# Attention outputs of a unit in one step and two PSUM banks, with the last keys' four products on the four quarters of TensorE

## The chip, the cores and the metric

The kernel runs on one NeuronCore of a Trainium2 chip. The metric is the device time of one execution in microseconds (us), as the median of several runs. The engines are named as in the profile: PE is TensorE (PEld its weight loads), DVE is VectorE, ACT is ScalarE, POOL is GpSimd, SP is SyncE. PE writes its results into PSUM banks; ACT here moves them to SBUF.

## The reference

Two blocks follow each other. The first is attention that keeps only the 32 best keys of every query, for 8 batches of 8 heads with 576 positions and 64 dimensions:

```python
scores = scale * np.matmul(q, k.transpose(0, 1, 3, 2))
kth = np.partition(scores, -top_k, axis=-1)[..., -top_k:-top_k + 1]
scores = np.where(scores >= kth, scores, -1000000000.0)
attn = np.exp(scores - np.max(scores, axis=-1, keepdims=True))
attn = attn / (np.sum(attn, axis=-1, keepdims=True) + 1e-09)
x = np.matmul(attn, v)
```

The second sends each of the 4608 rows of `x` (512 wide) to the one expert of eight with the largest logit, computes `relu(x @ w1[e]) @ w2[e]` there (512 to 1024 to 512), and scales the row with the gate's probability. Everything is float32.

## The kernel before

**Units, tiles, steps.** A unit is a pair of heads: the 128 partitions hold 64 dimensions of each, so there are 8 x 4 = 32 units. The 576 queries of a head are four tiles of 128 and a tail of 64. One step of the main loop (`loop`, 144 steps) works on two score tiles side by side, the same tile number of both heads; the two tails of an even and of the odd unit behind it form one step together. So two units take nine steps. By their place in these nine, steps 0 to 3 are the tiles of the even unit, step 4 is the tails, steps 5 to 8 are the tiles of the odd unit (`groups`, line 252).

**What a step does.** DVE searches the 32nd largest score of each query (`fold`, `fold_on`, `search`). ACT then forms `low` from the threshold (line 401) and a mask term with two Relu passes (line 417); POOL subtracts it from the scores (`less`, line 426); ACT takes the exponential (line 434). PE turns the weights of the step before (`transposed`: eight transposes `wTm`, line 445, and one or two for the last 64 keys, `wTl`, lines 459 and 461), ACT copies them out of PSUM (`wT`, lines 450 and 452; `wTt`, lines 467 and 469), and PE makes the scores of the step four ahead (`products`, line 304), which ACT copies to `s` (line 311) one step later.

**Order of work.** The order on PE, ACT and DVE is the program order of `loop`, written by hand; POOL's operations are held in program order too (`in_turn`). Within a step ACT's order is: `low`, Relu, copies of scores, then what is due at the place "relu" (copies of outputs), copies of turned weights, exponentials, and last the copy of `wTt`. PE's order is: the eight transposes, some pieces, the transpose for the last keys, more pieces, the scores, what is due at the place "products" (outputs), and the rest of the pieces. A piece is a fragment of the expert blocks, four matmuls of line 979 or one of line 996; `share` decides how the pieces that a step may have are spread over the places of the nine, and a step's share is cut in three by `part = min(BETWEEN, now - now // 2)` and `now // 2`. What is left of the experts' work runs after the loop, on PE alone.

**Outputs.** When a unit's weights are turned, `outputs` multiplies them with V. For each half of 288 queries there are five chunks of keys and two heads: ten matmuls, each 64 output rows wide, so that the two heads stand on the two column halves of the array. The fifth chunk is the last 64 keys of both heads, one head above the other on the partitions; V has zeros in its place for the other head, so that a product over all 128 partitions gives one head's sum (`_laid_out`). Each half takes one bank, ACT copies it to `oT` (line 484), and later five products with a turning matrix (`px`, line 493) bring rows and logits. `ending` places these: for the even unit the first half at the end of step 3 and the second at the end of step 5; for the odd unit at the end of step 8 and of the next step 0; `px` is one step after the second half.

**Banks.** Outputs, turned weights, `px` and the ranks of the gate share one pool of two banks (`bank`, tag "t"). Each new user waits until the copy out of the bank two users ago is done.

Of the kernel before, what the change touches and what calls it, by code (L numbers as in the profile page):

```python
# [44 lines left out]
def kernel(  # L45
# [205 lines left out]

    def groups(u):

        first, second = ([((a, i), (a, NC + i)) for i in range(NC)] for a in (u, u + 1))
        return first + [((u, 2 * NC), (u + 1, 2 * NC))] + second

    def in_turn(put):
# [14 lines left out]

    def tails(tiles):
        return tiles[0][1] == 2 * NC

    def tail_at(n):
        return 0 if n.u % 2 else S
# [80 lines left out]
    def search(tiles, s, f, then=lambda: None, soon=False, behind=lambda: None, beside=lambda: None):  # L358

        m_all = range(2)  # L360
        tops = k.small.tile([P, 2, TOP_K], F32, name="tops", bufs=4)
        if k.exact:
            src = [s[:, m, :, :].rearrange("p j k -> p (j k)") for m in m_all]
            width = S
        else:
            src = [f.few[:, m, 0:QF] for m in m_all]
            width = LW
            if not f.aside:
                lists(f)
        behind()  # L370
        scr = k.att.tile([P, 2, width], F32, name="scr", bufs=1)
        nbias = k.small.tile([P, 2], F32, name="nbias", bufs=3)
        R = TOP_K // 8

        for r in range(R):
            if r == R - 1 and not soon:
                then()
            for m in m_all:
                nc.vector.max(out=tops[:, m, r * 8:(r + 1) * 8], in_=src[m])  # L379
                if r > 1:  # L380
                    tick()
            if r == 1 and soon:
                then()
            if r == 0:
                in_turn(nc.gpsimd.tensor_scalar_mul(nbias, tops[:, :, 0], -scale))
                beside()
            if r < R - 1:
                for m in m_all:
                    first = r == 0 and not k.exact
                    nc.vector.match_replace(  # L390
                        out=src[m] if first else scr[:, m, :], in_to_replace=tops[:, m, r * 8:(r + 1) * 8],
                        in_values=src[m], imm_value=NEG,
                    )
# [7 lines left out]
        nc.scalar.activation(low, thr, AF.Copy, scale=STEEP)  # L401

        def doubts():
            n, i = tiles[0]
# [25 lines left out]
    def weights(tiles, w, nbias):  # L430

        for m, (n, i) in enumerate(tiles):
            c = 2 * NC if tails(tiles) else 2 * tiles[0][1] + m
            nc.scalar.activation(  # L434
                w[:, m, :], w[:, m, :], AF.Exp, scale=scale, bias=nbias[:, m:m + 1], accum_out=n.z[:, c:c + 1]
            )

    def transposed(tiles, w):

        q = slice(ST + tiles[0][1] * P, ST + (tiles[0][1] + 1) * P)  # L440
        for m, (n, i) in enumerate(tiles):
            pm = bank("wTm")
            for c in range(NC):
                first = c * P + (0 if tails(tiles) else m * ST)
                nc.tensor.transpose(pm[:, c * P:(c + 1) * P], w[:, m, first:first + P], ident)  # L445
            pm4 = pm[:, :].rearrange("p (c q) -> p c q", c=NC)
            if tails(tiles):
                at = tail_at(n)
                pmh = pm4.rearrange("p c (h q) -> p c h q", h=2)
                nc.scalar.copy(wT[:, :, :, at:at + ST], _turned(pmh, 2) if m else pmh)  # L450
            else:
                nc.scalar.copy(wT[:, :, m, q], pm4)  # L452
                if k.between and not m:
                    yield
        yield
        pt = bank("wTl")
        if tails(tiles):
            for a in range(2):
                nc.tensor.transpose(pt[0:ST, a * P:(a + 1) * P], w[:, 1 - a, SM:S], ident)
        else:  # L460
            nc.tensor.transpose(pt[:, 0:P], w[:, :, :].rearrange("p m k -> p (m k)")[:, SM:SM + P], ident)
        yield
        if tails(tiles):
            pt4 = pt[0:ST, 0:2 * P].rearrange("p (r q) -> p r q", q=ST)
            for h in range(2):
                both = wTt[h * ST:(h + 1) * ST, :].rearrange("p (a q) -> p a q", q=ST)[:, 0:NT + 1:NT, :]
                nc.scalar.copy(both, pt4[:, 0:4:3, :] if h else pt4[:, 1:3, :])
        else:
            nc.scalar.copy(wTt[:, q], pt[:, 0:P])

    def outputs(n, x):

        odd = n.u % 2
        oT = oT_of[odd]
        for j in range(2):
            q = slice(j * HF + (0 if odd else ST), (j + 1) * HF + (0 if odd else ST))
            po = bank("po")
            for c in range(KC):
                for h in range(2):
                    r = slice(h * D, (h + 1) * D)  # L480
                    rhs = wT[:, c, h, q] if c < NC else wTt[:, q]
                    nc.tensor.matmul(po[r, 0:HF], n.v[:, c, r], rhs, start=(c == 0), stop=(c == KC - 1))  # L482
            yield
            nc.scalar.copy(oT[:, j * HF:(j + 1) * HF], po[:, 0:HF])  # L484
            yield
        starts = [t * P + (ST if odd else 0) for t in range(NC)] + [0 if odd else SM]
        xw = P + lw
        n.xl = k.small.tile([P, KC, xw], F32, name="xl", bufs=1)
        put = []
        for t0, t1 in ((0, KC - 2), (KC - 2, KC)):  # L490
            px = bank("px")
            for t in range(t0, t1):
                nc.tensor.matmul(
                    px[:, (t - t0) * xw:(t - t0 + 1) * xw], oT[:, starts[t]:starts[t] + P],
                    turn[:, n.u // 2, odd * lw:odd * lw + xw], start=True, stop=True,
                )
# [527 lines left out]
    with fast:  # L1024
# [86 lines left out]
        def ending(b, u):  # L1111
# [6 lines left out]
                lg_of[b] = k.small.tile([P, KC, E], F32, name="lg")  # L1118
            x, lg = x_of[b], lg_of[b]
            out_steps = outputs(n, x)  # L1120
            yield "products"
            next(out_steps)
            yield "relu"
            next(out_steps)
            if u % 2 == 0:
                yield "relu"
            div = divisors(n)
            next(div)
            aside.append(div)
# [95 lines left out]
        def multiply(i):  # L1225
            tiles = tiles_of(i)
            got_of[i] = products(tiles, i < AHEAD)
            n, tile = tiles[0]
            more = n.b * U + n.u + 2
            if tile == (NC - 1 if n.u % 2 else 2 * NC) and more < len(units):  # L1230
                unit.append(load_unit(*units[more]))

        def loop():
# [15 lines left out]
            fold_on(f_of[0])  # L1249
            for i, (b, g) in enumerate(work):  # L1250
                tiles = tiles_of(i)
                u, tile = g[0]
# [37 lines left out]
                if b == B - 1 and at >= ARRIVED:  # L1290
                    room -= KEEP
                    credit = room / (len(work) - i)
                share = {0: 0.5, 1: 1.2, 2: 1.6, 3: 0.5, 2 * NC: 1.4}[tile]
                now = max(0, min(int(credit * share + 0.5), room))
                credit -= now
                clock = i
# [29 lines left out]
            assert len(late) == 1  # L1326
            clock = None
            for place in late[0][0]:
                if place == "rows":
                    pieces(4)  # L1330
            kept = left - (SURE + HALVES + PLAIN) * PIECES
            assert kept >= 0, kept
            k.apart = True
# [24 lines left out]
    with ExitStack() as outer:  # L1358
# [10 lines left out]
        with ExitStack() as st:  # L1369
# [7 lines left out]
            with tc.For_i(0, B, 1) as b:  # L1377
# [3 lines left out]
                for u in range(0, U, 2):  # L1381
# [4 lines left out]
                    for g in groups(u):  # L1386
# [10 lines left out]
                        n, tile = tiles[0]  # L1397
# [33 lines left out]
def _laid_out(inputs):  # L1431
# [5 lines left out]
    T = S % P  # L1437
    qt, kt = (a.transpose(0, 1, 3, 2).reshape(B, U, P, S) for a in (q, k))
    vt = v.reshape(B, U, 2, S, D).transpose(0, 1, 3, 2, 4)
    vp = _np.zeros((B, U, S + T, 2, D), v.dtype)  # L1440
    vp[:, :, :S - T] = vt[:, :, :S - T]
    for h in range(2):
        vp[:, :, S + (h - 1) * T:S + h * T, h] = vt[:, :, S - T:, h]
    return {
        "qk": _np.concatenate([qt, kt[..., -T:], kt], axis=3),
        "v": vp.reshape(B, U, S + T, P),
# [27 lines left out]
```

## Time and profile before

| | |
|---|---|
| median of 3 runs | 1282.69 us (1282.21 to 1283.14) |
| the profiled execution | 1284.61 us, its span 1283.0 us |
| 20 to 220 us: PE, DVE, ACT busy | 142.09, 200.00, 168.28 us; PE clock 0.85 |
| 220 to 470 us | 227.38, 249.76, 217.51 us of 250; clock 0.96 |
| 470 to 1050 us | 567.76, 575.55, 495.94 us of 580; clock 1.00 |
| 1050 to 1283 us | 226.38, 18.24, 44.75 us of 233; clock 1.00 |

The first row of stages is attention alone, the next two are attention with the pieces of experts between it, the last is experts alone. The times of PE's matmuls overlap, and their ends are modelled, so the distance from one start to the next says what a matmul costs.

### The profile page before, as it was taken

The numbers are of one execution on the slowest core, as the hardware profiler recorded it, in microseconds if no ns is written. First come the engines' busy times: TensorE is split into PE (matmuls) and PEld (weight loads), VectorE is DVE, ScalarE is ACT, GpSimd is POOL, SyncE is SP. The second block draws the span as 40 slices with busy tenths as digits, with TensorE's granted clock in tenths as the row PEclk, the third lists the DMA queues.
The fourth block names the chain that finished last, engine by engine and source line by source line (L and its number), as shares of the span: only waits on it lengthen the run. The fifth ranks groups of instructions, "written<-read, shape, count | busy, mean of one in ns | idle before, by whom it ended". The sixth has DMA issues, their size and how long they took to land. (4 is left out here: it accounts for less than half of the span.)

```text
span 1283.0 us, 24461 instructions
## 1 busy us (share of the span) xinstructions
PE 1176.1 (92%) x7574; PEld 823.6 (64%) x7574; DVE 1058.8 (83%) x4608; ACT 933.3 (73%) x2136; POOL 732.0 (57%) x884
## 2 busy tenths in 40 slices
PE   6767767898899999999999999999999999999998
PEld 3444444665566566667666666666666667789975
DVE  8999999999999999999999999999999965000000
ACT  4888887988799888888788888888888872112121
POOL 4777777786678665658555855676557743101010
PEclk9888788999899999999999999999999999999999
DMA  5001113741474147533946464547555548996582
GB/s 153 31 30 31 31 39 126 263 157 39 146 251 162 39 150 283 182 135 98 332 142 218 163 224 153 189 146 264 178 178 202 172 149 285 353 358 235 215 301 83
DMA packets 98701, 220.81 MB, mean 172 GB/s; under 512 B 5309, under 2 KB 26301, under 8 KB 98560
## 3 DMA queue, kind: packets, MB, share of 16 engines
q1 hardware_dynamic: 91360, 198.87, 44.5%
q0 software_dynamic: 6384, 19.97, 4.2%
q8 instruction: 61, 1.00, 0.3%
q14 instruction: 80, 0.66, 0.2%
q10 hardware_dynamic: 816, 0.31, 0.1%
HBM read 195.75 MB, written 24.04 MB: 171 GB/s over the span
## 5 line engine op out<-in xcount | busy, mean ns | idle before, releaser
L426 POOL TENSOR_TENSOR w<-s,w 128x576 f32<-128x576 f32 x288 | 409.2, 1441 | 317.5 <-ACT w L417 317.4
L979 PE MATMUL ph<-xTs,w 128*128 128x128 f32 x2112 | 263.0, 278 | 2.6 <-ACT xTs L870 2.6
L979 PEld LDWEIGHTS ph<-xTs,w 128*128 128x128 f32 x2112 | 251.3, 194 | 21.1 <-issue 17.6
L996 PE MATMUL py<-w,hT 128*128 128x512 f32 x528 | 248.7, 600 | 1.9 <-ACT hT L984 1.6
L434 ACT ACTIVATE w<-w,nbias 128x576 f32<-128x576 f32 x288 | 223.0, 785 | 2.3 <-POOL w L426 1.4
L445 PE MATMUL wTm<-turn,w 128*128 128x128 f32 x1152 | 173.9, 291 | 52.7 <-ACT oT L484 29.1
L417 ACT ACTIVATE w<-s,low 128x576 f32<-128x576 f32 x288 | 207.7, 768 | 4.7
L304 PE MATMUL sc<-qkb 64*128 64x288 f32 (+1 forms) x1280 | 200.7, 465 | 7.8 <-DMA qkb<-in_qk_dram 4.0
L445 PEld LDWEIGHTS wTm<-turn,w 128*128 128x128 f32 x1152 | 135.1, 148 | 111.6 <-ACT oT L484 35.5
L311 ACT COPY s<-sc 128x576 f32<-128x576 f32 x288 | 168.0, 634 | 11.9 <-PE sc L304 11.8
L379 DVE MAX8 tops<-scr 128x8 f32<-128x168 f32 x576 | 169.5, 328 | 0.0
L452 ACT COPY wT<-wTm 128x512 f32<-128x512 f32 x256 | 140.7, 596 | 37.8 <-PE wTm L445 37.2
L379 DVE MAX8 tops<-few 128x8 f32<-128x144 f32 (+1 forms) x576 | 154.9, 314 | 0.0
L304 PEld LDWEIGHTS sc<-qkb 64*128 64x128 f32 (+1 forms) x1280 | 107.1, 190 | 71.5 <-issue 35.2
L996 PEld LDWEIGHTS py<-w,hT 128*128 128x128 f32 x528 | 92.0, 191 | 86.5 <-issue 83.0
L482 PE MATMUL po<-wT,vb 128*64 128x288 f32 x1024 | 143.8, 425 | 0.0
L888 POOL DMA_INDIRECT out_dram<-y,xg x37 | 38.9, 1052 | 161.3 <-ACT y L1005 82.0
L356 DVE MAX8 few<-l 128x8 f32<-128x288 f32 x288 | 129.8, 451 | 0.0
L320 DVE TENSOR_TENSOR h<-s 128x576 f32<-128x576 f32 (+1 forms) x145 | 111.7, 770 | 3.9 <-ACT s L311 3.6
L321 DVE TENSOR_TENSOR l<-s 128x576 f32<-128x576 f32 (+1 forms) x145 | 114.3, 788 | 0.0
L482 PEld LDWEIGHTS po<-wT,vb 128*64 128x64 f32 x1024 | 70.1, 141 | 68.9 <-issue 17.4
L356 DVE MAX8 few<-hl 128x8 f32<-128x72 f32 x576 | 102.3, 221 | 0.0
(205 smaller groups left out, 1596.7 us busy)
## 6 DMA issues: line engine op xcount, KB each, us to landing
w<-in_moe_w_dram SPq DMA_DIRECT2D x74, 2048.0 KB, 9.2
qkb<-in_qk_dram SPq DMA_DIRECT2D x31, 608.0 KB, 3.8
vb<-in_v_dram SPq DMA_DIRECT2D x32, 320.0 KB, 3.2
xg<-x_rows SPq DMA_DIRECT2D x37, 257.0 KB, 9.1
x_rows<-blank SPq DMA_DIRECT2D x13, 257.0 KB, 7.9
x_rows<-blank POOLq DMA_DIRECT2D x4, 257.0 KB, 9.8
x_rows<-x,posi POOLq DMA_INDIRECT x40, 3.2
out_dram<-y,xg POOLq DMA_INDIRECT x37, 3.9
```

The source lines that it names most:

```text
L304: nc.tensor.matmul(ps[rows, j, 0:HF], n.q[d, cols], n.k[d, keys], start=True, stop=True)
L311: lambda m=m, ps=ps: nc.scalar.copy(s[:, m, :, :], ps[:, :, 0:HF]) for m, ps in enumerate(got)
L356: nc.vector.max(out=f.few[:, m, QF + 8 * j:QF + 8 * j + 8], in_=away)
L379: nc.vector.max(out=tops[:, m, r * 8:(r + 1) * 8], in_=src[m])
L417: nc.scalar.activation(w[:, m, :], s[:, m, :, :].rearrange("p j k -> p (j k)"), AF.Relu, scale=-STEEP, bias=low[:, m:m + 1],)
L426: k.last_pool = in_turn(nc.gpsimd.tensor_tensor(w[:, m, :], s[:, m, :, :].rearrange("p j k -> p (j k)"), w[:, m, :], op=ALU.subtract)).ins
L434: nc.scalar.activation(w[:, m, :], w[:, m, :], AF.Exp, scale=scale, bias=nbias[:, m:m + 1], accum_out=n.z[:, c:c + 1])
L445: nc.tensor.transpose(pm[:, c * P:(c + 1) * P], w[:, m, first:first + P], ident)
L452: nc.scalar.copy(wT[:, :, m, q], pm4)
L482: nc.tensor.matmul(po[r, 0:HF], n.v[:, c, r], rhs, start=(c == 0), stop=(c == KC - 1))
L979: nc.tensor.matmul(ph[:, f, :], n.w1[:, 0, dt, fc * P:(fc + 1) * P], n.xT[:, dt, :], start=(dt == 0), stop=(dt == DT - 1),)
L996: nc.tensor.matmul(py, hT[:, f, :], n.w2[:, 0, f, :], start=(f == 0), stop=(f == FT - 1))
```

## The change

In `outputs` both halves are now made in one place, in two banks. The halves are no longer equal: they meet at query 256 of the tiles, so one is 256 columns wide and the other 320. The products of the last keys come first. For the first half, head 0's keys lie on the lower partitions; for the second half the heads are exchanged, which `groups` arranges by listing the two tiles of places 2, 3, 7 and 8 in the other order. So the four products (two halves, two heads) each use 64 partitions and 64 columns, a different quarter of the array, and V needs no zeros: its last chunk is laid out once more as it is. Both copies to `oT` follow together one step later. `ending` waits one or two places "weights" instead of making the first half, so the even unit's outputs are made at the end of step 5 and the odd unit's at the end of step 0; `px` stays where it was. The shares of the pieces change: places 0 and 5 go from 0.5 to 0.1, 3 and 8 from 0.5 to 1.2, the tails from 1.4 to 1.2, 1 and 6 from 1.2 to 1.1, 2 and 7 from 1.6 to 1.5. For the tails the transposes of the last keys take all 128 columns and land on partitions 64 to 127. After the loop a piece stands at each place "products".

```diff
     def groups(u):
-        first, second = ([((a, i), (a, NC + i)) for i in range(NC)] for a in (u, u + 1))
+        first, second = (
+            [((a, i), (a, NC + i))[::-1 if i >= NC // 2 else 1] for i in range(NC)] for a in (u, u + 1)
+        )
...
     def outputs(n, x):
...
-        for j in range(2):
-            q = slice(j * HF + (0 if odd else ST), (j + 1) * HF + (0 if odd else ST))
+        halves = []
+        middle = ST + SM // 2
+        for j, (q0, q1) in enumerate(((0 if odd else ST, middle), (middle, S if odd else S + ST))):
             po = bank("po")
-            for c in range(KC):
+            halves.append((po, q0, q1))
+            for h in range(2):
+                r, keys = (slice(a * D, (a + 1) * D) for a in (h, h ^ j))
+                nc.tensor.matmul(
+                    po[r, 0:q1 - q0], n.v[keys, NC, r], wTt[keys, q0:q1], start=True, stop=False
+                )
+        for po, q0, q1 in halves:
+            for c in range(NC):
                 for h in range(2):
                     r = slice(h * D, (h + 1) * D)
-                    rhs = wT[:, c, h, q] if c < NC else wTt[:, q]
-                    nc.tensor.matmul(po[r, 0:HF], n.v[:, c, r], rhs, start=(c == 0), stop=(c == KC - 1))
-            yield
-            nc.scalar.copy(oT[:, j * HF:(j + 1) * HF], po[:, 0:HF])
-            yield
+                    nc.tensor.matmul(
+                        po[r, 0:q1 - q0], n.v[:, c, r], wT[:, c, h, q0:q1], start=False, stop=(c == NC - 1)
+                    )
+        yield
+        for po, q0, q1 in halves:
+            at = 0 if odd else ST
+            nc.scalar.copy(oT[:, q0 - at:q1 - at], po[:, 0:q1 - q0])
+        yield
...
     def ending(b, u):
...
-            yield "products"
-            next(out_steps)
+            for _ in range(1 if u % 2 else 2):
+                yield "weights"
             yield "relu"
-            next(out_steps)
-            if u % 2 == 0:
-                yield "relu"
...
-                share = {0: 0.5, 1: 1.2, 2: 1.6, 3: 0.5, 2 * NC: 1.4}[tile]
+                share = {0: 0.1, 1: 1.1, 2: 1.5, 3: 1.2, 2 * NC: 1.2}[tile]
...
             for place in late[0][0]:
-                if place == "rows":
-                    pieces(4)
+                pieces({"products": 1, "rows": 4}.get(place, 0))
...
-    vp = _np.zeros((B, U, S + T, 2, D), v.dtype)
-    vp[:, :, :S - T] = vt[:, :, :S - T]
-    for h in range(2):
-        vp[:, :, S + (h - 1) * T:S + h * T, h] = vt[:, :, S - T:, h]
+    vp = _np.concatenate([vt, vt[:, :, S - T:]], axis=2)
```

The rest of the diff names a tile's place with `place_of`, so that the sums of the weights, `wT` and `doubt` are still stored at their own places, and takes the tails' last keys from partitions 64 to 127 of the bank.

More of the change, by code (lines that the diff above doesn't have):

```diff
@@ L274, in tails, with place_of @@
         return tiles[0][1] == 2 * NC
+    def place_of(tile):
+        return tile if tile == 2 * NC else tile % NC
     def tail_at(n):
@@ L403, in doubts @@
         def doubts():
-            n, i = tiles[0]
+            n, i = tiles[0][0], place_of(tiles[0][1])
             at = n.b * U + n.u
@@ L432, in weights @@
         for m, (n, i) in enumerate(tiles):
-            c = 2 * NC if tails(tiles) else 2 * tiles[0][1] + m
+            c = 2 * NC if tails(tiles) else 2 * place_of(i) + i // NC
             nc.scalar.activation(
@@ L438, in transposed @@
     def transposed(tiles, w):
-        q = slice(ST + tiles[0][1] * P, ST + (tiles[0][1] + 1) * P)
+        at = ST + place_of(tiles[0][1]) * P
+        q = slice(at, at + P)
         for m, (n, i) in enumerate(tiles):
@@ L451, in transposed @@
             else:
-                nc.scalar.copy(wT[:, :, m, q], pm4)
+                nc.scalar.copy(wT[:, :, i // NC, q], pm4)
                 if k.between and not m:
@@ L458, in transposed @@
             for a in range(2):
-                nc.tensor.transpose(pt[0:ST, a * P:(a + 1) * P], w[:, 1 - a, SM:S], ident)
+                nc.tensor.transpose(pt[:, a * P:(a + 1) * P], w[:, 1 - a, S - P:S], ident)
         else:
@@ L463, in transposed @@
         if tails(tiles):
-            pt4 = pt[0:ST, 0:2 * P].rearrange("p (r q) -> p r q", q=ST)
+            pt4 = pt[P - ST:P, 0:2 * P].rearrange("p (r q) -> p r q", q=ST)
             for h in range(2):
                 both = wTt[h * ST:(h + 1) * ST, :].rearrange("p (a q) -> p a q", q=ST)[:, 0:NT + 1:NT, :]
-                nc.scalar.copy(both, pt4[:, 0:4:3, :] if h else pt4[:, 1:3, :])
+                nc.scalar.copy(both, pt4[:, 1 - h:4 - h:2, :])
         else:
@@ L1227, in multiply @@
             got_of[i] = products(tiles, i < AHEAD)
-            n, tile = tiles[0]
+            n, tile = tiles[0][0], place_of(tiles[0][1])
             more = n.b * U + n.u + 2
@@ L1251, in loop @@
                 tiles = tiles_of(i)
-                u, tile = g[0]
+                u, tile = g[0][0], place_of(g[0][1])
                 if tile == 0 and u % 2 == 0:
@@ L1396 @@
                             pass
-                        n, tile = tiles[0]
+                        n, tile = tiles[0][0], place_of(tiles[0][1])
                         if tile == (NC - 1 if n.u % 2 else 2 * NC):
```

## The prediction

> **What bounds the kernel now.** I read the page's slices first (40 of 32.1 us each).
>
> ```profile
> PE   6767767898899999999999999999999999999998
> ...
> DVE  8999999999999999999999999999999965000000
> ...
> PEclk9888788999899999999999999999999999999999
> ```
>
> DVE is full until 1050 us and PE from 490 us on; before 230 us PE has room and half of its clock at times; after 1060 us PE is alone and, by the waits, idle only once (0.45 us, for the ranks). So the loop ends when DVE's chain does, and every us lost there moves the end by one. Then the list of waits.
>
> ```profile
> ACT low L401 <- DVE tops L379: 41.5, 50, 2.8
> ...
> PEld wTm L445 <- ACT oT L484: 35.5, 29, 3.7
> ...
> DVE h L320 <- ACT s L311: 3.6, 4, 1.6
> ```
>
> DVE hardly ever waits. But `low`, which needs DVE's threshold, waits for DVE in only 50 of 144 steps: in the others ACT comes late. What that costs is in the timeline around steps 14 and 15.
>
> ```profile
> 117.32 3.54 PE L482 MATMUL po<-wT,vb 128*64 128x288 f32 x16
> ...
> 120.69 0.65 PE L482 MATMUL po<-wTt,vb 128*64 128x288 f32 x4
> ...
> 121.39 0.40 ACT L484 COPY oT<-po 128x288 f32<-128x288 f32 x1 [1.08 <-PE po L482]
> ...
> 121.97 1.16 ACT L452 COPY wT<-wTm 128x512 f32<-128x512 f32 x2 [0.18 <-PE wTm L445]
> ...
> 124.69 0.21 ACT L401 ACTIVATE low<-tops 128x2 f32<-128x2 f32 x1
> ...
> 125.78 2.77 POOL L426 TENSOR_TENSOR w<-s,w 128x576 f32<-128x576 f32 x2 [1.99 <-ACT w L417]
> ...
> 128.03 0.84 DVE L327 TENSOR_TENSOR few<-h 128x288 f32<-128x288 f32 x1
> ```
>
> ACT waits for a half of the outputs, then copies, then exponentials; `low` starts at 124.69 though DVE's last MAX8 of the threshold ended at 124.09. So POOL's subtraction ends at 128.55, and DVE's L327, which takes 0.45 elsewhere, takes 0.84 until POOL is done. With `low` in time POOL ends just as L327 starts (both 114.86 a step earlier). L327 averages 557 ns over 144: about 16 us lost there.
>
> **The Trainium skill.** SBUF — State Buffer, "Who interferes with whom": a DVE instruction with two SBUF inputs and a GpSimd one that reads SBUF exclude each other for the whole instruction; the 0.84 agrees. TensorEngine Tiling (Array Packing), "Key Properties": tiles run independently, a change of mode drains the array. The trace agrees: the tails' scores on 64*64 start four at a time within 21 ns, and a change costs some 0.10 leaving and 0.05 entering. TensorE: Matmul & The Clock Gate, "What's actually happening": half clock until some 3.4 us of activity; here pairs of output products start every 0.48 us, later every 0.24.
>
> **PE's work per unit.** A half now: 10 matmuls, 20 rows in the trace, a pair every 0.242, 2.42 + 0.15 for modes = 2.58 (903.03 to 905.61 below); a unit 5.15. After: the quarters, 8 rows by fours, two starts of the width 320: 2 x 0.269 = 0.54; the other 16 matmuls, 32 rows in pairs, 8 x 0.215 + 8 x 0.269 = 3.87; two modes 0.30. Sum 4.71: 0.44 saved, 14 us over 32 units. The copies to `oT` move the same columns (0.40 a half): steps 4 and 0 lose one, steps 6 and 1, which had one, have two; the first can run while PE makes the second half. The tails' transposes are as many, their weight loads twice as wide (0.145 for 0.115, hidden under matmuls). V's loads keep their place, bytes and queue, SP's, and the order built for DVE is unchanged; on POOL some output stores stand a step later, behind the subtraction instead of ahead of it, at about 1 us each either way. These I cost at nothing: the cover is DVE's own step, and without it the stores, some six, could give or take 1 us each. The pieces up to the loop's end differ by one.
>
> **The wait it adds.** The quarters come first, so PE waits for `wTt`, ACT's last copy of the step. Before, it was needed last in a half. One late step 5:
>
> ```profile
> 899.82 1.04 PE L445 MATMUL wTm<-turn,w 128*128 128x128 f32 x8
> ...
> 900.45 1.07 ACT L450 COPY wT<-wTm 128x512 f32<-128x512 f32 x2 [1.14 <-PE wTm L445]
> 900.69 1.02 PE L996 MATMUL py<-w,hT 128*128 128x512 f32 x2
> 901.55 0.38 PE L459 MATMUL wTl<-turn,w 128*64 128x128 f32 x2
> ...
> 901.86 1.24 PE L304 MATMUL sc<-qkb 64*128 64x288 f32 x8
> ...
> 903.03 2.16 PE L482 MATMUL po<-wT,vb 128*64 128x288 f32 x16
> 903.09 0.51 ACT L467 COPY wTt<-wTl 64x128 f32<-64x128 f32 x2
> ...
> 905.61 1.25 PE L445 MATMUL wTm<-turn,w 128*128 128x128 f32 x8
> ```
>
> From the first transpose the copies of `wTt` land 3.78 later (3.4 where it is one copy). PE alone needs less: `wTl` needs the bank of the first `wT` copy (1.2 after the start), the scores and their modes 1.48 more, so the quarters are ready at 2.65. PE idles 0.75 to 1.1 there. It idles 0.4 more ahead of `wTl`: the piece (0.86) that filled this is gone, since with the share 0.1 the built order has no piece in steps 0 and 5 for 31 of 32 units. Together 1.3 a unit. Queued behind it on PE are both halves, and behind them the next step's transposes, for which ACT waits, then `low`, POOL, and DVE.
>
> **Where PE is full** (17 units, 470 to 1050): +1.3, -0.44, and -0.43 for bank waits that go with the half in step 8 (step 0 from 927.60 takes 7.45; its parts, transposes 0.98, two pieces 1.72, scores 1.28, a half 2.58, come to 6.6). Net +0.43 x 17 = 7; as DVE sets the pace in part of it, I take 4. Ends: -8 (no new wait: -0.45 each) to +9.
>
> **Where PE is not full.** Steps 14/15 with the change: both halves start at 117.32, `wTt` has landed. Quarters at half clock 1.2, then four pairs of 256 columns at 0.425 until 120.2, then 4 x 0.215 + 8 x 0.269 = 3.0, leaving 0.1: end 123.3 instead of 121.27. `low` follows 3.42 after that end: 126.7, 2.6 late instead of 0.6. POOL's passes run from 127.8 to 130.6, L327 at 128.03 loses 1.2 instead of 0.39, and as ACT has no slack in the next step (`low` to `low` 6.75 us, against a period of 7.3 that had the loss in it) a second loss of about 0.9 follows. That is +1.7; with full clock at the start the end is 122.0, `low` 1.3 late, +0.7. Middle 1.2 x 6 units before 220 us = 7 (0 to 12). For the 8 units from 220 to 470 the clock is up but the quarters wait: start 5.9 after the threshold, end 4.0 into the next step of 6.55, `low` about 0.9 late, 0.75 lost, against 0.4 in steps 6 and nothing in most steps 1: +0.5 x 8 = 4 (0 to 8).
>
> **The end.** The half in front of the last turn moves behind it, with one piece at each place "products": PE is busy throughout, so only the saved 0.44 counts.
>
> **Sum.** 7 + 4 + 4 - 0.4 = +15 on the profiled span of 1283.0. The profiled execution was 1284.6, 1.9 over the median; the same difference on the median 1282.7 gives 1297.5.
>
> **Rivals.** (a) Faster: PE is the bound from 470 us and takes the saving, because `wTt` is there in time. Then 17 x 0.45 = -8 and nothing early: 1275. For it: PE busy 567.76 of 580. It decides if the wait at the quarters is below 0.4 us a unit; against it, in most steps 0 and 5 of the trace the copy lands 0.1 to 0.8 after the outputs start, even with a piece ahead. (b) No difference: DVE sets the pace (575.55 of 580 busy), and neither saving nor wait reaches it: 1282.5. Against it: L327's length depends on ACT's lateness. (c) The quarters don't run side by side, so that the change doesn't do what it says: 0.54 more a unit, another 17 x 0.5 = 9: 1306. Against it: the four starts of the tails' scores. (d) Mild: losses at the lower ends, +3 to +8: 1288.
>
> **Chances.** Main case (1291 to 1304) 0.50, (d) 0.20, (c) or losses beyond the main case 0.08, (b) 0.08, (a) 0.14. A measurement of this kernel tells some 0.2%, 2.6 us, from no change: slower 0.78, same 0.08, faster 0.14. Range: leaving out the farthest of (a) and of (c), 1279 to 1308; main case's own 1291 to 1304.
>
> **What would show it.** Right: PE idle before `po` on the copy of `wTt` (0.7 to 1.1, some 25 times); one start of four rows at the quarters; `low` 1 to 3 us late in steps 2 and 7 before 470 us; L327 with more stretched instances; the first step after 1050 us later by the whole difference; the last stage unchanged. Wrong: L327's mean at or under 557 ns, or no idle time at the quarters.

## The result: 5.1% slower, and the profile after

The changed kernel takes 1346.95 us (median, 1346.1 to 1352.15), the kernel before 1282.45 us beside it. The ratio is 1.0511, 95% interval 1.0487 to 1.0534: 65 us lost where the prediction had 15. The profiled execution has a span of 1346.1 us, against 1283.0.

The slices of the changed kernel's page (40 of 33.7 us each, tenths busy):

```profile
PE   6777667898989898989899999999999999999998
...
DVE  8999999999999999999999999999999983200000
...
PEclk9678978899999899999999999999999999999999
```

DVE now runs until about 1105 us, and PE is no longer at 9 throughout from 490 us on: slices of 8 and 9 alternate until about 670 us. Neither engine has more instructions (7574 of PE and 4608 of DVE in both kernels), so something makes them pause or slows them. The list of waits of the changed kernel (us in total, times, longest; PEld is PE loading weights):

```profile
PE wTl L467 <- ACT wT L458: 82.9, 39, 4.9
ACT oT L501 <- PE po L495: 78.7, 54, 3.4
...
ACT low L406 <- DVE tops L384: 34.8, 32, 2.8
...
DVE h L325 <- ACT s L316: 13.6, 18, 1.5
...
PEld wTm L451 <- ACT oT L501: 4.0, 19, 0.4
```

Before, PE waited 26.2 us at `wTl`, ACT 21.3 us at `oT`, and `PEld wTm <- ACT oT` was 35.5. PE and ACT now wait for each other in turn. `low` waits for DVE in only 32 steps, so ACT is late in the other 112, and DVE's L327 (now L332), which the prediction had named for this, gets longer; its group, with the mean in ns behind the busy time:

```profile
L332 DVE TENSOR_TENSOR few<-h 128x288 f32<-128x288 f32 x144 | 92.2, 640 | 0.0
```

640 ns in place of 557. Where the time goes by stage, read from the start of DVE's first fold of steps 30, 66 and 143 and the end of the span: +6.2 us up to step 30 (209.9 to 216.1), +12.2 in steps 30 to 65 (255.6 to 267.8), +39.2 in steps 66 to 142 (570.1 to 609.3), +5.5 after (247.4 to 252.9). The third stage is where the question lies. A step 8 and the step 0 behind it, there, in the timeline of the kernel before (start, duration, engine, line; what ended an idle time in brackets):

```profile
858.02 1.24 PE L304 MATMUL sc<-qkb 64*128 64x288 f32 x8
...
859.19 2.16 PE L482 MATMUL po<-wT,vb 128*64 128x288 f32 x16
...
861.18 0.66 PE L482 MATMUL po<-wTt,vb 128*64 128x288 f32 x4
861.77 1.22 PE L445 MATMUL wTm<-turn,w 128*128 128x128 f32 x8
...
862.83 1.88 PE L996 MATMUL py<-w,hT 128*128 128x512 f32 x4
863.66 1.06 ACT L452 COPY wT<-wTm 128x512 f32<-128x512 f32 x2
...
864.55 0.27 PE L461 MATMUL wTl<-turn,w 128*128 128x128 f32 x1
```

The same place in the changed kernel:

```profile
907.56 1.24 PE L309 MATMUL sc<-qkb 64*128 64x288 f32 x8
...
908.34 0.26 ACT L475 COPY wTt<-wTl 128x128 f32<-128x128 f32 x1
...
908.74 1.12 PE L1013 MATMUL py<-w,hT 128*128 128x512 f32 x2
...
909.70 1.04 PE L451 MATMUL wTm<-turn,w 128*128 128x128 f32 x8
...
910.50 1.15 ACT L316 COPY s<-sc 128x576 f32<-128x576 f32 x2
...
911.55 1.06 ACT L458 COPY wT<-wTm 128x512 f32<-128x512 f32 x2
...
912.19 0.33 PE L467 MATMUL wTl<-turn,w 128*128 128x128 f32 x1 [1.46 <-ACT wT L458]
912.45 1.20 PE L309 MATMUL sc<-qkb 64*64 64x288 f32 x16
...
913.47 0.70 PE L488 MATMUL po<-wTt,vb 64*64 64x320 f32 x4
...
914.17 0.24 ACT L475 COPY wTt<-wTl 128x128 f32<-128x128 f32 x1
...
914.47 0.65 PE L488 MATMUL po<-wTt,vb 64*64 64x256 f32 x4 [0.29 <-ACT wTt L475]
...
915.04 4.10 PE L495 MATMUL po<-wT,vb 128*64 128x320 f32 x32
...
917.47 0.42 ACT L501 COPY oT<-po 128x320 f32<-128x320 f32 x1 [1.47 <-PE po L495]
...
919.19 0.37 ACT L501 COPY oT<-po 128x256 f32<-128x256 f32 x1 [1.30 <-PE po L495]
```

Two things are to be seen. First, `wTl` cannot be written before ACT has copied the first `wT`, since that frees its bank, and ACT gets to that copy in its own time: it is not idle here, but works without a pause through `wTt`, `low`, Relu and the copies of scores, from 908.34 to 911.55. Before, PE came to it behind 2.58 us of outputs (859.19 to 861.77), the transposes and two pieces: at 864.55, when the first of the two copies that begin at 863.66 was through, and without idle time. Now it has one piece in place of the half and none behind the transposes, and stands idle for 1.46 us. Second, the four quarters are not made together: the first half's pair starts at 913.47, the second half's at 914.47, when `wTt` has landed. Only the second half's columns need that copy; the order on PE is the program's, and the pair that was ready went alone.

### The profile page after: what moved, and what is told of

It is laid out like the page before. It is cut to its first block, busy times and chain, and to the rows that moved or that the text cites. A ratio compares the mean times of both kernels' runs of the same rounds, so it can differ in the third digit from the quotient of the medians.

```text
span 1346.1 us, 24506 instructions
## 1 busy us (share of the span) xinstructions
PE 1196.2 (89%) x7574; PEld 832.9 (62%) x7574; DVE 1105.9 (82%) x4608; ACT 936.3 (70%) x2136; POOL 733.2 (54%) x884
## 5 line engine op out<-in xcount | busy, mean ns | idle before, releaser
L996 PEld LDWEIGHTS ph<-xTs,w 128*128 128x128 f32 x2112 | 252.8, 195 | 22.7 <-issue 19.4
L309 PE MATMUL sc<-qkb 64*128 64x288 f32 (+1 forms) x1280 | 209.7, 480 | 6.4 <-DMA qkb<-in_qk_dram 3.7
L451 PE MATMUL wTm<-turn,w 128*128 128x128 f32 x1152 | 171.2, 291 | 26.4 <-ACT xl L517 13.8
L316 ACT COPY s<-sc 128x576 f32<-128x576 f32 x288 | 168.2, 634 | 19.1 <-PE sc L309 18.9
L384 DVE MAX8 tops<-scr 128x8 f32<-128x168 f32 x576 | 165.2, 314 | 0.0
L309 PEld LDWEIGHTS sc<-qkb 64*128 64x128 f32 (+1 forms) x1280 | 112.4, 198 | 72.2 <-issue 36.4
L384 DVE MAX8 tops<-few 128x8 f32<-128x144 f32 (+1 forms) x576 | 151.1, 301 | 0.0
L495 PE MATMUL po<-wT,vb 128*64 128x256 f32 (+1 forms) x1024 | 136.6, 421 | 0.0
L361 DVE MAX8 few<-l 128x8 f32<-128x288 f32 x288 | 127.0, 441 | 0.0
L467 PE MATMUL wTl<-turn,w 128*128 128x128 f32 x128 | 40.1, 313 | 83.9 <-ACT wT L458 82.9
L495 PEld LDWEIGHTS po<-wT,vb 128*64 128x64 f32 x1024 | 72.9, 142 | 65.4 <-issue 22.7
## 6 DMA issues: line engine op xcount, KB each, us to landing
xg<-x_rows SPq DMA_DIRECT2D x37, 257.0 KB, 9.2
x_rows<-blank SPq DMA_DIRECT2D x13, 257.0 KB, 8.6
x_rows<-blank POOLq DMA_DIRECT2D x4, 257.0 KB, 8.4
```

The lines of the kernel that those rows point to most:

```text
L309: nc.tensor.matmul(ps[rows, j, 0:HF], n.q[d, cols], n.k[d, keys], start=True, stop=True)
L316: lambda m=m, ps=ps: nc.scalar.copy(s[:, m, :, :], ps[:, :, 0:HF]) for m, ps in enumerate(got)
L361: nc.vector.max(out=f.few[:, m, QF + 8 * j:QF + 8 * j + 8], in_=away)
L495: nc.tensor.matmul(po[r, 0:q1 - q0], n.v[:, c, r], wT[:, c, h, q0:q1], start=False, stop=(c == NC - 1))
L996: nc.tensor.matmul(ph[:, f, :], n.w1[:, 0, dt, fc * P:(fc + 1) * P], n.xT[:, dt, :], start=(dt == 0), stop=(dt == DT - 1),)
```

## Experiments

Four theories were set against each other. *ACT in order* (first form): ACT stands at two `oT` copies for both halves, and `low` behind them comes late. *Burst*: the 4.7 us of products in one step are more than a step holds. *Quarters*: PE's wait for `wTt`. *Shares*: the new spread of pieces. A fifth, *gap*, came from the first results: the first half had filled PE's time in front of `wTl`. A place is the step's number modulo nine, as in the kernel's description.

**The merge alone.** The kernel before, with both halves in one step:

```diff
-            yield
+            halves.append(po)
+        yield
+        for j, po in enumerate(halves):
             nc.scalar.copy(oT[:, j * HF:(j + 1) * HF], po[:, 0:HF])
-            yield
+        yield
...
-            yield "products"
-            next(out_steps)
+            for _ in range(1 if u % 2 else 2):
+                yield "weights"
```

> The kernel before with one thing of the change alone: both halves of a unit's outputs are made in one step into two banks, and their two copies to oT follow together; all ten matmuls of a half as before (zero-padded V, no quarters, last keys' product at the end of each half), old shares of pieces. ACT-in-order theory (the loss comes from ACT waiting for both halves at once, so that everything behind it, the threshold's `low` with it, comes late): at least 45 of the 64 us of loss, 1325 us or more. Quarters theory (the loss is PE waiting for `wTt` ahead of the quarters): 1280 to 1295. Shares theory: 1280 to 1290.

Measured: 1327.8 us, ratio 1.0338 (1.0308 to 1.0368), some 43 us of the 65. Its list of waits:

```profile
PE wTl L461 <- ACT wT L452: 86.9, 52, 4.3
...
ACT oT L487 <- PE po L483: 69.4, 44, 3.0
...
ACT low L401 <- DVE tops L379: 38.5, 41, 2.8
```

Both waits of the changed kernel are there without quarters and without new shares. So neither quarters nor shares can carry the main loss. This run does not say what of the merge costs, as it also takes the first half out of steps 3 and 8.

**All but the merge and the shares.** The changed kernel with the halves back in two steps, one bank each, old shares:

```diff
-            halves.append((po, q0, q1))
...
-        yield
-        for po, q0, q1 in halves:
+            yield
             at = 0 if odd else ST
...
-            for _ in range(1 if u % 2 else 2):
-                yield "weights"
+            yield "products"
+            next(out_steps)
```

> The changed kernel with the merge alone undone: the two halves of a unit's outputs are made in two steps and in one bank each, at the places of the kernel before, and with its old shares; kept are the exchanged heads, V without its zeros, the 256 and 320 columns, and the last keys' products on quarters, ahead of a half's column products, now two at a time (the same PE time as the pair they replace). Burst theory (PE's 4.7 us of products in one step of some 7 us, which then holds more than PE can do in a step, make ACT wait at the copies to oT, and ACT cannot catch up): within 10 us of the kernel before, 1278 to 1295. Quarters theory (the wait of the quarters for `wTt` is what costs): 1300 or more.

1304.74 us, ratio 1.0171 (1.0140 to 1.0201): more than the burst theory allowed, so the quarters (with the 256 and 320 columns and the exchanged heads, which this run keeps too) do cost something, about 20 us when they stand in front of each half. Most of it (+15.4 us) is in steps 66 to 142; PE idles 11.1 us there ahead of the quarters, and at `wTl` exactly as long as before, 7.2 us.

**The shares.** Once in the kernel before, once taken out of the changed one:

```diff
-                share = {0: 0.5, 1: 1.2, 2: 1.6, 3: 0.5, 2 * NC: 1.4}[tile]
+                share = {0: 0.1, 1: 1.1, 2: 1.5, 3: 1.2, 2 * NC: 1.2}[tile]
```

> The kernel before with the new shares of pieces per step (0.1, 1.1, 1.5, 1.2, 1.2) and nothing else. Burst theory: the shares are worth less than 10 us here, 1276 to 1293. Shares theory (the bunching of pieces in place 3 costs): 1300 or more.

> The changed kernel with the old shares of pieces per step (0.5, 1.2, 1.6, 0.5, 1.4 for places 0, 1, 2, 3 and the last keys). Shares theory (no piece in places 0, bunching in place 3): at least 25 us come back, 1320 or less. ACT-in-order and quarters theory: within 12 us of the changed kernel, 1335 to 1358; longer if the pieces ahead of the products push the halves later still.

1289.9 us, 1.0051 (1.0033 to 1.0070), and 1341.11 us, 1.0437 (1.0419 to 1.0454): the shares cost 6 to 10 us either way round, not 25.

**Quarters behind the columns**, so that `wTt` is needed last:

```diff
-            for h in range(2):
-                r, keys = (slice(a * D, (a + 1) * D) for a in (h, h ^ j))
...
+        for j, (po, q0, q1) in enumerate(halves):
+            for h in range(2):
+                r, keys = (slice(a * D, (a + 1) * D) for a in (h, h ^ j))
+                nc.tensor.matmul(
+                    po[r, 0:q1 - q0], n.v[keys, NC, r], wTt[keys, q0:q1], start=False, stop=True
+                )
```

> The changed kernel with the quarters moved behind the sixteen column products of the two halves, so that PE needs `wTt` last. ACT-in-order theory: at least 50 us of the loss stay, 1333 us or more. Quarters theory: at least 25 us come back, 1320 or less.

1339.81 us, 1.0433 (1.0409 to 1.0457): some 10 us back, the rest stays. PE's idle time at the quarters (5.7 us by the gaps in steps 66 to 142) is gone, but that at the next transposes rises from 7.9 to 14.9. In this order neither bank is finished until the very end, which fits but was not tested apart.

**ACT's copies later.** The description of the kernel says that output copies follow the copies of scores. That holds for steps 1 to 65 only; from step 66 on `loose` is false and they stand ahead of them, right behind the Relu passes. This run puts them behind everywhere:

```diff
-                if not loose:
-                    at_place("relu")
-                    at_place("rows")
...
-                if loose:
-                    at_place("relu")
+                at_place("relu")
+                if not loose:
+                    at_place("rows")
```

> The changed kernel with the two output copies of ACT put behind the scores' copies in every step, where before only steps 1 to 65 had them there and the later ones had them ahead of the scores' copies. ACT-in-order theory: ACT's wait for `po` falls by about one us in each of 17 late units, some 20 us come back, 1320 to 1335. Quarters theory and shares theory: no more than 5 us either way, 1341 to 1352.

1349.46 us, 1.0499 (1.0478 to 1.0519): nothing. ACT's wait at `oT` did fall, 78.7 to 64.4 us, and that at the copies of scores rose from 18.9 to 29.4. So the length of ACT's wait at `oT` is not what sets the time, and the theory falls in its first form; nothing shows that the late order, which my description had wrong, cost the prediction anything. The same edit in the kernel before:

> The kernel before with ACT's copies to oT behind the scores' copies in the late steps too (from step 66 on they stand ahead of them). In the late stage ACT idles 15 us at these copies. If that idle time limits the stage, 3 to 12 us less, 1271 to 1280; as PE is busy there all but 11 us of 570, at most what PE idles can come back, and as the same move brought nothing in the changed kernel, no difference is likeliest: 1279 to 1287.

1290.76 us, 1.0043 (1.0026 to 1.0059): a little slower, where no difference had been likeliest.

**Shorter products.** Two of the four column products of each half left out, in the changed kernel and, as a control, in the one before (there the loop over chunks is cut to `(0, NC - 1, NC)`, the last being the last keys):

```diff
-            for c in range(NC):
+            for c in (0, NC - 1):
```

> The changed kernel with two of the four column products of each half left out (chunks 1 and 2 of the keys), so that a unit's products take some 2.8 us of PE instead of 4.7; the outputs lack the values of those keys. Burst theory: with the burst short enough for its step the loss of the merge goes, so that the time falls by 50 us or more, 1255 to 1297, and the waits of ACT at the copies to oT fall from 79 to under 40 us. Theories without the burst (quarters, shares): 10 to 30 us less, as PE's work is less by 62 us, half of it in stretches where it is not the bound.

> The kernel before with the same two of four column products left out of each half, so that a half takes 1.6 us instead of 2.6; the outputs lack the values of those keys. It is the control of the run above. Burst theory: the difference between the two short kernels is under 20 us, against 64 for the full ones, and this one falls by 10 to 35 us. If instead the merge costs the same whatever the length of the burst (banks held longer, copies in one step), the two short kernels differ by 45 us or more.

The whole times, 1682.02 and 1654.63 us, say nothing: other outputs send rows to other experts, and what follows the loop took 631 and 628 us instead of 253 and 247. The loop itself holds the same pieces and can be compared. The start of step 143 is at 1048.9 against 1022.6 us, a difference of 26 where the full kernels have 58. So less than half is left with short products, but more than the burst theory's 20. Part of the reason is likely that PE has room there: in steps 66 to 142 of the short kernel before, PE idles 27.6 us, and DVE is busy for all 557.9 us. And one number did not move: PE idles 27.1 us at `wTl` in steps 66 to 142 of the short merged kernel, 26.6 in the full one, 27.2 in the merge alone, while ACT's wait at `oT` over the whole kernel is down to 23.8. A pause that does not depend on the length of the burst is not caused by it. By place, PE's idle time at `wTl` in steps 66 to 137, summed from the gaps between PE's records and divided by the number of such steps (us):

| kernel | place 0 | place 4 | place 5 |
|---|---|---|---|
| before | 0.32 | 0.12 | 0.14 |
| changed | 1.75 | 0.93 | 0.44 |
| merge alone | 1.73 | 1.03 | 0.14 |
| changed, short products | 1.75 | 0.99 | 0.45 |
| changed, halves split again | 0.32 | 0.12 | 0.14 |

Places 0 and 4 are those behind steps 8 and 3, where the first half used to be. That gave the gap theory, and two tests of it.

**Filling the gap.** The changed kernel with pieces moved from places 1, 2, 6 and 7 to 0 and 5:

```diff
-                share = {0: 0.1, 1: 1.1, 2: 1.5, 3: 1.2, 2 * NC: 1.2}[tile]
+                share = {0: 0.5, 1: 0.8, 2: 1.4, 3: 1.2, 2 * NC: 1.2}[tile]
```

> The changed kernel with other shares of pieces (0.5, 0.8, 1.4, 1.2, 1.2): one piece more between the transposes and `wTl` of places 0 and 5, one more behind the scores of places 3 and 8, fewer in places 1 and 6. Gap theory (the first half had filled PE's time in front of `wTl` in places 0 and 4, where PE now waits 1.75 and 0.93 us for ACT's copy of `wT`, whatever the length of the products): that wait falls by 8 us or more in the late stage, and the time by 8 to 20 us, 1327 to 1339. Burst theory (products and pieces of places 0 and 5 exceed the step): no gain, 1343 to 1360.

1327.34 us, 1.0330 (1.0313 to 1.0347): some 23 us back. The timeline of PE, same place:

```profile
896.42 1.12 PE L1013 MATMUL py<-w,hT 128*128 128x512 f32 x2
897.39 1.04 PE L451 MATMUL wTm<-turn,w 128*128 128x128 f32 x8
898.26 1.02 PE L1013 MATMUL py<-w,hT 128*128 128x512 f32 x2
899.87 0.33 PE L467 MATMUL wTl<-turn,w 128*128 128x128 f32 x1 [0.59 <-ACT wT L458]
```

One piece between the transposes and `wTl` takes the place of most of the idle time: 0.59 instead of 1.46 (over the steps of the table 1.07 instead of 1.75 in place 0, 0.67 instead of 0.93 in place 4). The share of 0.5 in place 0 does not do it alone: the changed kernel with the old shares has it too and idles 27.6 us at `wTl`; there places 3 and 8 have 0.5 instead of 1.2, and at the same place PE is through with the scores of step 8 by 4.6 us before `wTl`, here by 3.4. At `wTl` PE's idle time in steps 66 to 142 falls from 26.6 to 14.7 us, and that stage gets 17 us shorter. The burst theory, which had this edit load a step already too full, expected no gain; as the main cause it falls.

**Moving the half without merging.** The kernel before, halves in two steps and one bank each, but none of them in steps 3 and 8. The even unit's are made in steps 4 and 5, the odd unit's in 0 and 1, so that its second half and `px` come one step later than before:

```diff
             out_steps = outputs(n, x)
+            yield "weights"
             yield "products"
             next(out_steps)
             yield "relu"
             next(out_steps)
-            if u % 2 == 0:
-                yield "relu"
```

> The kernel before with its two halves still in two steps and one bank each, but none of them in places 3 and 8: they are made in places 4 and 5 of the first unit of a pair (before: 3 and 5) and 0 and 1 of the second (before: 8 and 0). Gap theory (what costs is that the half no longer fills PE's time in front of `wTl` in places 4 and 0): PE's idle time at `wTl` in the late stage rises from 7 to 20 us or more and the time by 8 to 25 us, 1292 to 1310. Merge theory (two halves in one step, ACT waiting for both, is what costs): PE's idle time at `wTl` stays and the time is 1279 to 1290.

1324.6 us, 1.0319 (1.0291 to 1.0347): 41 us lost with nothing merged, as much as the merge alone loses. That is more than the gap theory's 8 to 25; its count had the late stage alone, but in steps 30 to 65 PE's idle time at `wTl` rises too, from 3.0 to 19.1 us. The timeline at a step 8 and 0:

```profile
889.64 1.24 PE L304 MATMUL sc<-qkb 64*128 64x288 f32 x8
890.82 1.09 PE L445 MATMUL wTm<-turn,w 128*128 128x128 f32 x8
...
891.74 1.88 PE L996 MATMUL py<-w,hT 128*128 128x512 f32 x4
...
894.53 1.08 ACT L452 COPY wT<-wTm 128x512 f32<-128x512 f32 x2
...
895.17 0.33 PE L461 MATMUL wTl<-turn,w 128*128 128x128 f32 x1 [1.55 <-ACT wT L452]
```

PE is through with the transposes and both pieces by 893.6 and waits for ACT. The idle time averages 1.48 us in place 0 and 0.90 in place 4, close to the merged kernels. Of the 23.7 us that this kernel loses in steps 66 to 142, 16.0 are PE's idle time at `wTl`. In the first 30 steps the two differ: this kernel loses 2 us there, the merge alone 6, so where PE is not full the merge itself costs.

**The quarters.** Two orders of the products in the changed kernel: each half's pair directly ahead of its own columns (first diff), and all four between the two halves' columns (second; `cols` makes the sixteen products of one half).

```diff
-        for po, q0, q1 in halves:
             for c in range(NC):
```

```diff
+        cols(halves[0], True)
+        for j, (po, q0, q1) in enumerate(halves):
...
-                    po[r, 0:q1 - q0], n.v[keys, NC, r], wTt[keys, q0:q1], start=True, stop=False
+                    po[r, 0:q1 - q0], n.v[keys, NC, r], wTt[keys, q0:q1], start=bool(j), stop=not j
...
+        cols(halves[1], False)
```

> The changed kernel with each half's two quarters directly ahead of its own sixteen column products, so that the second half's quarters, which alone need the newest columns of `wTt`, come 2 us later and PE need not stop for them (in the changed kernel they start 1.0 to 1.5 us after the first half's in most units, not with them). Theory now: of the 57.6 us at the loop's end some 20 are this stop, about 1.0 us in each of 17 late units and less in the 14 before: 15 to 22 us less, 1325 to 1332. If the stop only hides a wait that PE then has elsewhere (at the next transposes): within 5 us, 1342 or more.

> The changed kernel with the order: the first half's sixteen columns products, the four quarters together, the second half's column products. `wTt` has then landed, so that nothing parts the four quarters, which then take about 0.7 us instead of 1.6 to 2.2. If the time of PE in that step counts in full: 12 to 22 us less than the changed kernel, 1325 to 1335. If it only hides a wait (as with the quarters by halves, where 0.4% came back): 1338 or more.

By halves: 1345.52 us, 1.0468 (1.0451 to 1.0485), only some 5 us less. PE no longer stops (its waits at `wTl` and at the next transposes stay as they were), but two pairs at 0.6 to 0.7 us each, with their changes of mode, cost nearly what the one stop did. Between: 1335.64 us, 1.0407 (1.0383 to 1.0431), some 13 us less, and its timeline of PE:

```profile
902.70 2.38 PE L488 MATMUL po<-wT,vb 128*64 128x320 f32 x16
905.00 0.76 PE L501 MATMUL po<-wTt,vb 64*64 64x320 f32 x8
905.69 1.95 PE L488 MATMUL po<-wT,vb 128*64 128x256 f32 x16
```

One group of eight rows, 0.69 us from start to start, in all units of the late stage; the first rows of all four start within some 20 ns. In the changed kernel the way from the first quarter to the first column product averages 1.68 us over the 17 units from 470 to 1060 us, and four rows start together in only 6 of all 32 units. This agrees with the Trainium skill (TensorEngine Tiling (Array Packing), "Key Properties": tiles run independently): the array can do it, if nothing in the queue parts the four.

**Both repairs together**, with the shares of the filled kernel:

> Both of the last two edits together. If the stop at the second half's quarters and the gap at `wTl` are separate losses, the gains add: 23 to 40 us less than the changed kernel, 1307 to 1324. If one makes room for the other: no more than the larger of the two alone.

> The last run's order together with the other shares (0.5, 0.8, 1.4, 1.2, 1.2), which brought the changed kernel some 20 us. If the two are separate: 1305 to 1317. If the other shares' gain and this one overlap, as with the quarters by halves: 1322 to 1332. Below 1284, faster than the kernel before, is not expected.

By halves 1330.35 us, 1.0351 (1.0334 to 1.0368), no better than the fill alone. Between 1316.95 us, 1.0253 (1.0229 to 1.0276): half of the loss is back, and the gains of fill and quarters add up to within 4 us. It is the best form of the change that was run; none is faster than the kernel before.

The stages of the runs that the argument rests on (us; PE idle is the sum of the gaps between its records in steps 66 to 142):

| kernel | to step 30 | 30 to 65 | 66 to 142 | after | PE idle, of it at `wTl` |
|---|---|---|---|---|---|
| before | 209.9 | 255.6 | 570.1 | 247.4 | 11.4, 7.2 |
| changed | 216.1 | 267.8 | 609.3 | 252.9 | 42.5, 26.6 |
| merge alone | 215.8 | 263.6 | 598.2 | 248.3 | 33.5, 27.2 |
| halves moved, not merged | 211.4 | 267.8 | 593.8 | 248.8 | 29.4, 23.2 |
| changed, halves split again | 210.9 | 257.0 | 585.5 | 248.5 | 22.7, 7.2 |
| changed, gap filled | 216.0 | 265.6 | 592.2 | 250.3 | 29.4, 14.7 |
| changed, quarters between | 216.6 | 265.0 | 600.4 | 249.5 | 36.2, 25.9 |

## Why the prediction was wrong

The direction was right, slower; the size was off by a factor of four, and the time lies outside the range. Of some 50 us missing, 35 are in the late stage. There the sum per unit was +1.3 of waits, −0.43 of waits given back and −0.44 of PE's work, +0.43 in all. Measured over the same 17 units: +1.9 of idle time and +0.4 of PE's busy time, +2.3 in all. The two terms that were booked as gains did not come, and the waits were larger than the 1.3.

**The step that failed: "−0.43 for bank waits that go with the half in step 8".** Taking the half out of step 8 was booked as time given back, and the wait that it would open was put at nothing. The runs show the opposite. The half stood in a place where PE would have waited for ACT in any case, so a good part of its 2.58 us had been free: without it PE idles 1.4 us more in place 0 and 0.8 more in place 4. The 0.43 had been got as a remainder (half of 7.45 measured minus 6.6 for the parts of a step), and the remainder was misread. The step it was taken from, at 927.60 in the kernel before, shows what it is:

```profile
930.12 0.33 PE L461 MATMUL wTl<-turn,w 128*128 128x128 f32 x1 [0.44 <-ACT wT L452]
```

Of the 0.85 us, 0.44 are PE waiting at `wTl` for ACT's copy of `wT`, the very wait that then grew, and 0.26 are `wTl` itself (the scores behind it start at 930.38), which the list of parts had left out. Waits for banks at the transposes, where the prediction's line `PEld wTm <- ACT oT` would count, leave PE idle for only 1.2 us in all of steps 66 to 142.

The "0.4 more ahead of `wTl`" that I did book was for the missing piece in steps 0 and 5. That is about what the new shares alone do in the kernel before (place 0 from 0.32 to 0.74, place 5 from 0.14 to 0.31); places 0 and 4 were not looked at as neighbours of the half that was taken away.

**"As DVE sets the pace in part of it, I take 4" of 7.** Wrong too: none of the loss was absorbed. In steps 66 to 142 of the kernel before PE is idle for 11 us of 570, but DVE is busy for 568, so the busy shares do not name one bound. The short kernel before helps: with 28 us less PE busy there, its stage is only 12 us shorter, and DVE is busy throughout. So PE held the stage some 12 us above what DVE needs, an estimate from these two runs, and a loss on PE comes on top. In the changed kernel PE's idle time rose by 32.5 us (31.1 in the table, which leaves out a pause across the end of the stage) and its busy time by 6.7, which is all of the 39 us. DVE pays the same 39 in its own way, 28.8 us of longer operations and 10.5 of idle time; 13 of the longer ones are L332 and L340, the two that read only `h`. POOL's part in them was not tested.

**PE's work, 4.71 us a unit.** Right as a price: the quarters take 0.69 to 0.70 when they run together (predicted 0.54 and their modes), the columns 4.04 (915.04 to 919.08) against 3.87. But the saving of 0.44 never came: they run together in only 6 of 32 units, and the merge alone, with the products of the kernel before, already has PE busy 6.0 us longer in that stage (see the end).

**The wait for `wTt`, 0.75 to 1.1 a unit.** The size is right: 1.68 minus 0.69, 1.0 us a unit. Its form is not. I had all four quarters behind the wait; in fact the first pair runs while the second waits, so that the wait and the lost parallelism of rival (c) are one event. Putting the quarters between the columns gave 9 us of that stage back, not 17. PE's idle time elsewhere did not grow in return (25.9 us at `wTl` instead of 26.6, 7.9 at the next transposes in both), so why the rest did not come back is open.

**The early units, +7.** Measured +6.2, by the mechanism named. The timeline of the changed kernel around steps 14 to 16:

```profile
120.66 1.34 PE L488 MATMUL po<-wTt,vb 64*64 64x256 f32 x8
...
121.93 5.30 PE L495 MATMUL po<-wT,vb 128*64 128x256 f32 x32
...
127.28 0.42 ACT L501 COPY oT<-po 128x320 f32<-128x320 f32 x1 [1.78 <-PE po L495]
...
130.61 0.20 ACT L406 ACTIVATE low<-tops 128x2 f32<-128x2 f32 x1
```

The products start as long after the threshold as before (6.5 us after, 6.4 before) and take 6.6 us where I had 6.0; `low` starts 3.2 us after its own threshold where I had 2.6. Here the sum was right step by step, and it is the merge that costs: alone it loses 5.9 in these steps.

**The middle units, +4.** Measured +12.2, above the predicted 0 to 8. Here I took the start of the products from the kernel before; the halves that left steps 3 and 8 open the gaps of places 4 and 0 here too (place 4: 2.5 us in the merge alone, 3.6 in the changed kernel, none before; place 0: 2.8, 2.3, none), and the products of the even unit begin 6.9 to 7.4 us after the threshold where I had 5.9. `low` is then 1.9 to 3.7 us late in the steps of place 7; in those of place 2 it is 0.5 to 1.4 late, as the 0.9 predicted.

**The end, −0.4.** Measured +5.5 after the start of step 143. The new shares alone bring 2.3 of it (249.7); the rest is open.

**Signs.** Seen: L327's mean above 557 ns; `low` late in places 2 and 7; nearly the whole loss (57.6 of 63 us) at the start of the last step. Half seen: PE's stop at the quarters, but between their pairs in most units, and 22 times in the list of waits. Not seen: one start of four rows in most units; an unchanged last stage.

What stays open: the merge itself (ACT waiting for two halves at once) costs some 4 us more than the moved half in the first 30 steps. In the late stage the filled kernel with the quarters between still loses 15 us; 7.5 of PE's idle time at `wTl` and about 8 at the transposes are left there, and these were not taken apart further.

## What to carry to other kernels

Before work is moved out of a step, ask what its engine would have done there: work that stands in front of a wait can be partly free, and where it goes away the wait comes out. A wait of zero in the profile may only mean that something fills it. When several small matmuls are to run side by side, look at what each of them waits for; one late operand parts the group where the queue keeps the program's order.

## What was not expected of the hardware

- Quarters that are next to each other in PE's queue run as a group of four (0.69 us) or as two pairs (mostly 1.6 to 2.2 us, at the ends 1.2 and 3.1) depending on one copy of ACT that only the second pair needs.
- The merge alone has the same matmuls as the kernel before, yet PE was busy 564.7 instead of 558.7 us in steps 66 to 142, with the granted clock at 0.98 instead of 1.00 between 470 and 1030 us. The other runs of the table go the same way: 1.00 where PE idles 11 or 23 us in that stage, 0.98 where it idles 29 us or more. That the pauses lower the clock fits this, but was not tested.
